# The small power-of-two products move from the output products' PSUM bank to columns of the transposes' banks

## The chip, the cores and the metric

One Trainium2 chip, one core. The metric is device time in microseconds; a kernel's time is the median of its runs. The engines are named as the profile names them: PE (TensorE, its matmuls), PEld (its weight loads), DVE (VectorE), ACT (ScalarE), POOL (GpSimd) and SP (SyncE, which here only issues DMAs).

## What is computed

Attention with a position bias, followed by a gated feed-forward block, all in fp32 (4 batches, 8 heads, 576 positions, head size 64; then 2304 tokens, 512 to 1536 to 512):

```python
scores = scale * np.matmul(q, k.transpose(0, 1, 3, 2))
x = (psi_rel / psi_i)[..., None]                       # log distances of positions
bias = np.maximum(x @ w1 + b1, 0.0) @ w2
scores = scores + bias.transpose(2, 0, 1)[None]
attn = np.exp(scores - np.max(scores, axis=-1, keepdims=True))
attn = attn / (np.sum(attn, axis=-1, keepdims=True) + 1e-09)
out = np.matmul(attn, v)                               # -> x: tokens by 512
return ((x @ w_a) * (x @ w_b)) @ w_out
```

## The kernel before

Attention goes by units (a batch, a pair of heads, one of two chunks of the queries), each cut into tiles of 128 queries by 576 keys. One generator, `attn_steps` (line 576), takes one step per tile `n` in two halves. The first half: `soft1(n)` (line 465; DVE line 472 adds the bias to the scores in PSUM and takes the extreme of each row, ACT line 477 takes the exponential), loads and preparations for coming units, and one step of `v_scale` (line 189). The second half: the scores of the next tile (`qk`, line 428, or `qk_pair`, line 450), `turn(n-2)` (line 514: five transposes of a finished tile on PE), where a unit is complete its output product (`pv_first`, line 480, or `pv`, line 547), and `soft2(n-1)` (line 500: POOL scales a tile by the reciprocal of its row sum).

`turn` allocates a PSUM tile `tp` of [128, 5, 128] fp32 from a pool with one buffer; PE fills its five columns of 128, then ACT copies all five to fp16 (line 538; for the first four units one plain copy, line 526), and DVE subtracts that copy to get the low parts (line 539 for columns 0 to 3, line 540 for partitions 64 to 127 of column 4). An output product fills a `pv` tile of [128, 512] fp32, also one buffer, which ACT (line 495 or 567) and then DVE (line 496 or 569) read out.

The weights of the feed-forward block and the values `v` are scaled by powers of two that are found on the chip. For that, ten times in all (six pairs of weight chunks, four batches of `v`), two small products are made: `pow2_down` (line 62) turns a column of maxima, one to four wide, into rows by a product with the identity (line 64, output 1 or 4 partitions by 128), DVE reduces it (line 66) and makes a small diagonal (lines 67 to 72); some steps later `pow2_up` (line 75) spreads that over 128 partitions by a product with ones (line 77, output 128 by 1 or 4), and DVE copies it out (line 79). Both take a `pv` tile under the name `pr`: they share the one buffer of the output products.

The weight steps (`wab_steps`, line 297: ACT and DVE build fp32 weights from 64-bit words, lines 244 to 249; ACT sums the absolute values, line 266; POOL and ACT split them into fp16 parts, lines 283 to 287), the feed-forward blocks (`moe_block`, line 635, products `ab` line 649; `moe_out`, products `o` line 698) and the attention steps are merged by count (lines 789 to 836). The order of PE's instructions is the order of the program (line 747). The order on the other engines is made by a planner from its own estimates; the program only adds that some instructions stay behind others (`late`, line 172) and that some loads stay behind the bias loads (`paced`, line 165). Waits between engines are put in by the framework from what each instruction reads and writes.

PSUM has eight banks of 512 fp32 values per partition: the scores take two, `tp` two, `pv` one, and three more the bias and first units at first and the feed-forward products later.

Of the kernel before, what the change touches and what calls it, by code (L numbers as in the profile page):

```python
# [7 lines left out]
F32 = mybir.dt.float32  # L8
# [39 lines left out]
def attention_moe(ctx, tc, q0d, q1d, kd, vd, idn, wp, wa, wb, wo, lsw, lg, rl, out):  # L48
# [8 lines left out]
    g_d = dram.tile([FC, 128, TOK], F32, name="g_d")  # L57
    winv = cst.tile([128, FC, 2], F32, name="winv")
    xt, cpool, epool, xpool = [], [None], [None], [None]
    vsc = []  # L60

    def pow2_down(mx, n, tag):
        ps = pvp.tile([128, 512], F32, tag="pv", name="pr")
        nc.tensor.matmul(ps[0:n, 0:128], mx, tab["idn"], start=True, stop=True)
        m = att.tile([n, 1], F32, tag="p2m" + tag, name="p2m", bufs=2)
        nc.vector.reduce_max(out=m, in_=ps[0:n, 0:128], axis=AX.X)
        nc.vector.tensor_scalar(out=m, in0=m, scalar1=3.0e38, scalar2=2.0 ** -100, op0=ALU.min, op1=ALU.max)
        nc.vector.tensor_scalar(
            out=m.bitcast(I32), in0=m.bitcast(I32), scalar1=0x7F800000, scalar2=None, op0=ALU.bitwise_and
        )  # L70
        dg = att.tile([n, n], F32, tag="p2d" + tag, name="p2d", bufs=2)
        nc.vector.tensor_scalar(out=dg, in0=tab["idn"][0:n, 0:n], scalar1=m, scalar2=None, op0=ALU.mult)
        return dg

    def pow2_up(dg, n, tag):
        ps = pvp.tile([128, 512], F32, tag="pv", name="pr")
        nc.tensor.matmul(ps[:, 0:n], tab["one"][0:n, :], dg, start=True, stop=True)
        g = att.tile([128, n], F32, tag="p2g" + tag, name="p2g", bufs=2)
        nc.vector.tensor_copy(g, ps[:, 0:n])
        return g  # L80
# [108 lines left out]
    def v_scale(b):  # L189
        mx = att.tile([128, NP], F32, tag="vmx", name="vmx", bufs=2)  # L190
        vfs = [load_v(b, hp) for hp in range(2)] if b else []
        yield
        for hp in range(NP):
            if b:
                junk = vf = vfs[hp]
            else:
                vf = st["vs", hp].rearrange("p x j d -> p (x j d)")
                junk = att.tile([128, 640], F32, tag="rv", name="junk", bufs=2)
            with late():
                nc.scalar.activation(junk, vf, AF.Abs, accum_out=mx[:, hp:hp + 1])  # L200
            junk = vf = None
            if b:
                vfs[hp] = None
                if hp + 2 < NP:
                    vfs.append(load_v(b, hp + 2))
            yield
        m1 = att.tile([128, 1], F32, tag="vm1", name="vm1", bufs=2)
        nc.vector.reduce_max(out=m1, in_=mx, axis=AX.X)
        dg = pow2_down(m1, 1, "v")
        yield  # L210
        if b:
            yield
        vsc.append(v_scales(pow2_up(dg, 1, "v"), b))
        yield
# [82 lines left out]
    def wab_steps(wt):  # L297
# [10 lines left out]
        for s in range(4 * np_ + 7):  # L308
            p, c = divmod(s - 7, 4)
            if 0 <= p < np_:  # L310
                if c == 0:
                    rms[p] = wab_scale(p, pow2_up(dgs.pop(p), 4, "w"))
                with late():
                    wab_parts(p, c, wfs.pop(s - 7), rms[p])
            p, c = divmod(s - 5, 4)
            if 0 <= p < np_ and c == 0:
                dgs[p] = pow2_down(ms.pop(p), 4, "w")
            if 1 <= s <= 4 * np_:
                p, c = divmod(s - 1, 4)
                if c == 0:  # L320
                    ms[p] = att.tile([128, 4], F32, tag="wm", name="wm", bufs=2)
                wab_size(2 * p + c // 2, c % 2, wfs[s - 1], ms[p])
            if s < 4 * np_:
                wfs[s] = wab_conv(*raws.pop(s))
                if s % 4 == 1 and s // 4 + 1 < np_:
                    fetch(s // 4 + 1)
            yield
# [186 lines left out]
    def turn(n, pool):  # L514
        u, t = TILES[n]
        c = UNITS[u][2]
        p = st.pop(("pn", n))
        tp = pool.tile([128, 5, 128], F32, tag="tp", name="tp", bufs=1)
        for x in range(5):
            c0 = min(128 * x, S - 128)  # L520
            nc.tensor.transpose(tp[:, x, :], p[:, c0:c0 + 128], tab["idn"])  # L521
        if u < NP:
            if t[0] == "A":
                st["pt", u] = epool[0].tile([128, 5, 256], F32, tag="pt", name="ptf", bufs=2)
            o = 128 * (t[0] == "B")
            evs.append(nc.scalar.copy(st["pt", u][:, :, o:o + 128], tp))
            return
        W = 512 + 128 * c
        if t in ("A0", "A2"):
            st["pt", u] = cpool[0].tile([128, 9, W], F16, tag="pt", name="pt", bufs=2)  # L530
        pt = st["pt", u]
        if t == "T":
            dst = pt.rearrange("p x (h w) -> p x h w", h=2)[:, :, :, 0:64]
            src = tp.rearrange("p x (h w) -> p x h w", h=2)
        else:
            o = {"A0": 0, "A1": 128, "B0": 256, "B1": 384, "A2": 64, "A3": 192, "B2": 384, "B3": 512}[t]
            dst, src = pt[:, :, o:o + 128], tp
        nc.scalar.copy(dst[:, 0:5], src)  # L538
        nc.vector.tensor_tensor(out=dst[:, 5:9], in0=src[:, 0:4], in1=dst[:, 0:4], op=ALU.subtract)  # L539
        nc.vector.tensor_tensor(  # L540
            out=dst[0:64, 4], in0=src[64:128, 4], in1=dst[64:128, 4], op=ALU.subtract
        )
# [33 lines left out]
    def attn_steps():  # L576
        vgen = [None]
        for n in range(NT + 3):
# [42 lines left out]
            if n >= 2 and n - 2 < NT:  # L621
                turn(n - 2, tpp)
# [120 lines left out]
    chunk_pool(0)  # L743
    qkp = ctx.enter_context(tc.tile_pool(name="qk0", bufs=1, space=PSUM))
    tpp = ctx.enter_context(tc.tile_pool(name="tp0", bufs=1, space=PSUM))
    pvp = ctx.enter_context(tc.tile_pool(name="pv0", bufs=1, space=PSUM))
    ctx.enter_context(tc.manual_schedule(engines={mybir.EngineType.PE}))
    wstack = ctx.enter_context(ExitStack())
# [140 lines left out]
```

## Time and profile before

| | |
|---|---|
| median of 3 runs | 876.42 us (870.93 to 877.58) |
| the profiled execution | 875.48 us, span 873.4 us |
| mean granted TensorE clock, of full speed | 0.945 |
| PE busy | 780.3 us (89%), 5936 matmuls |
| PEld busy | 622.9 us (71%) |
| DVE busy | 546.0 us (63%) |
| ACT busy | 512.5 us (59%) |
| POOL busy | 308.4 us (35%) |

The span is the time from the first to the last recorded instruction of the profiled execution. The busy time of an engine is the sum of its instructions; matmuls are pipelined, so a busy PE is not PE at its peak. In the timeline each row is a run of like instructions: the start in us from the span's start, the time that they took, the engine, the line, the operation, what is written from what, tile sizes, how many, and in brackets how long the engine was idle just before and whose end it then had waited for.

### The profile page before, as it was taken

The numbers are of one execution on the slowest core, as the hardware profiler recorded it, in microseconds if no ns is written. First come the engines' busy times: TensorE is split into PE (matmuls) and PEld (weight loads), VectorE is DVE, ScalarE is ACT, GpSimd is POOL, SyncE is SP. The second block draws the span as 40 slices with busy tenths as digits, with TensorE's granted clock in tenths as the row PEclk, the third lists the DMA queues.
The fourth block names the chain that finished last, engine by engine and source line by source line (L and its number), as shares of the span: only waits on it lengthen the run. The fifth ranks groups of instructions, "written<-read, shape, count | busy, mean of one in ns | idle before, by whom it ended". The sixth has DMA issues, their size and how long they took to land.

```text
span 873.4 us, 16482 instructions
## 1 busy us (share of the span) xinstructions
PE 780.3 (89%) x5936; PEld 622.9 (71%) x5936; DVE 546.0 (63%) x1291; ACT 512.5 (59%) x1102; POOL 308.4 (35%) x480
## 2 busy tenths in 40 slices
PE   5865669878888698988999999999999999999998
PEld 1244446647777466765888888888898898888886
DVE  5545577879799667765587778777787665210100
ACT  4747557857686467764577667766776666331310
POOL 0022446747366412321244433432443344220210
PEclk9959688969998799999999999999999999999999
DMA  7897265724776345443444444444443432100001
GB/s 214 242 298 237 77 217 185 208 60 126 232 231 186 91 141 163 139 120 100 127 126 130 130 139 147 118 133 137 117 121 125 127 87 65 55 2 25 1 10 39
DMA packets 52596, 114.16 MB, mean 131 GB/s; under 512 B 5156, under 2 KB 9508, under 8 KB 52516
## 3 DMA queue, kind: packets, MB, share of 16 engines
q1 hardware_dynamic: 44336, 97.34, 36.9%
q10 hardware_dynamic: 8180, 15.77, 6.1%
q8 instruction: 47, 0.77, 0.4%
q14 instruction: 33, 0.27, 0.1%
HBM read 95.91 MB, written 17.18 MB: 129 GB/s over the span
## 4 chain that ended last, share of the span: by engine, by line
PE 66%; DVE 11%; DMA 10%; ACT 6%; issue 4%; SPq 1%; POOL 1%; ACTq 0%; DVEq 0%; POOLq 0%
PE ab L649 25%; PE o L698 17%; PE tp L521 8%; PE qk L444 8%; PE pv L555 5%; PE psta L136 3%; DMA rv<-vd 2%; DMA wraw<-wb 2%; DVE p L472 2%; DMA bias<-bias_d 2%; ACT p L477 1%; DVE ks L373 1%; DVE wt L246 1%; DVE wt L249 1%; DMA rvf<-vd 1%
## 5 line engine op out<-in xcount | busy, mean ns | idle before, releaser
L649 PEld LDWEIGHTS <-w16t 128*128 128x128 f16 x2592 | 254.1, 99 | 44.2 <-issue 12.7
L649 PE MATMUL ab<-x,w16t 128*128 128x256 f16 x2304 | 276.5, 277 | 0.0
L472 DVE CUSTOM_DVE_ANT_0 p<-qk,bias 128x576 f32<-128x576 f32 x144 | 108.7, 755 | 90.4 <-PE tp L521 80.1
L508 POOL TENSOR_SCALAR p<-p,rc 128x576 f32<-128x576 f32 x144 | 126.5, 879 | 70.9 <-DVE rc L506 64.2
L538 ACT CAST pt<-tp 128x640 f16<-128x640 f32 x128 | 88.3, 690 | 101.9 <-PE tp L521 101.4
L477 ACT ACTIVATE p<-p,mn 128x576 f32<-128x576 f32 x144 | 111.7, 776 | 47.6 <-DVE mn L472 45.3
L521 PE MATMUL tp<-idn,p 128*128 128x128 f32 x720 | 111.7, 289 | 20.3 <-DVE pt L540 8.1
L505 POOL TENSOR_SCALAR rr<-sm 128x1 f32<-128x1 f32 x144 | 31.2, 217 | 278.0 <-ACT p L477 274.8
L698 PE MATMUL o<-wos,gh 128*128 128x512 f32 x384 | 124.4, 405 | 0.0
L674 POOL TENSOR_TENSOR gl<-g,gh 128x256 fp32r<-128x256 f32 x96 | 72.6, 758 | 132.0 <-ACT gh L673 130.8
L521 PEld LDWEIGHTS tp<-idn,p 128*128 128x128 f32 x720 | 87.8, 148 | 39.0 <-issue 19.9
L539 DVE TENSOR_TENSOR pt<-tp,pt 128x512 f16<-128x512 f32 x128 | 88.0, 688 | 8.6 <-ACT pt L538 8.3
L659 DVE SCALAR_TENSOR_TENSOR g<-ab,wv,asb 128x256 f32<-128x256 f32 x84 | 40.3, 482 | 82.2 <-ACT asb L657 80.9
L698 PEld LDWEIGHTS o<-wos,gh 128*128 128x128 f32 x384 | 69.1, 190 | 17.8 <-issue 5.4
L444 PE MATMUL qk<-ks,qs 128*128 128x288 f32 x384 | 73.2, 313 | 4.9 <-DVE mn L472 3.8
L698 PE MATMUL o<-wos,gl 128*128 128x512 f32 x192 | 75.8, 395 | 0.0
L136 PE MATMUL psta<-h,w2s 128*32 128x288 f32 (+17 forms) x352 | 48.7, 558 | 25.4 <-ACT bo L154 12.2
L444 PEld LDWEIGHTS qk<-ks,qs 128*128 128x128 f32 x384 | 57.3, 192 | 10.5 <-DVE mn L472 5.3
L657 ACT ACTIVATE asb<-ab,wv 128x256 f32<-128x256 f32 x84 | 39.2, 468 | 40.4 <-PE ab L649 40.3
L673 ACT CAST gh<-g 128x256 fp32r<-128x256 f32 x96 | 38.7, 405 | 35.1 <-DVE g L659 34.8
L555 PE MATMUL pv<-pt,vs 128*64 128x320 f16 (+1 forms) x784 | 56.5, 298 | 0.0
L126 DVE TENSOR_SCALAR h<-u,lgs 128x576 f32<-128x576 f32 (+17 forms) x117 | 46.4, 456 | 14.9 <-PE psta L136 14.5
(92 smaller groups left out, 977.0 us busy)
## 6 DMA issues: line engine op xcount, KB each, us to landing
bias<-bias_d SPq DMA_DIRECT2D x128, 288.0 KB
rv<-vd SPq DMA_DIRECT2D x40, 320.0 KB
bias_d<-bo ACTq DMA_DIRECT2D x36, 295.5 KB
rk<-kd SPq DMA_DIRECT2D x24, 288.0 KB
wraw<-wa SPq DMA_DIRECT2D x12, 512.0 KB
wraw<-wb SPq DMA_DIRECT2D x12, 512.0 KB
wraw<-wo SPq DMA_DIRECT2D x12, 512.0 KB
rq<-q1d SPq DMA_DIRECT2D x16, 320.0 KB
```

Of the source, the lines that this page charges most:

```text
L136: nc.tensor.matmul(dst[32 * g:32 * g + 32], tab["w2"], hs[g][:, c0:c1], start=True, stop=True)
L444: nc.tensor.matmul(ps[:, hf, :HB], a, b[:, hf * HB:hf * HB + HB], start=(x == 0), stop=(x == len(prods) - 1))
L472: ttr = nc.vector.tensor_tensor_reduce(out=p.rearrange("p (a n) -> p a n", a=2), in0=ps[:, :, :HB], in1=bt.rearrange("p (a n) -> p a n", a=2),
L477: exps.append(nc.scalar.activation(p, p, AF.Exp, bias=mn, scale=-1.0, accum_out=sm))
L508: nc.gpsimd.tensor_scalar(out=p, in0=p, scalar1=rc, scalar2=1.0, op0=ALU.mult, op1=ALU.mult)
L521: nc.tensor.transpose(tp[:, x, :], p[:, c0:c0 + 128], tab["idn"])
L538: nc.scalar.copy(dst[:, 0:5], src)
L539: nc.vector.tensor_tensor(out=dst[:, 5:9], in0=src[:, 0:4], in1=dst[:, 0:4], op=ALU.subtract)
L555: nc.tensor.matmul(ps[64 * j:64 * j + 64, :N], vs[:, part, vb, j, :], pt[:, pb, j * N:j * N + N], start=(x == 0), stop=(x == len(TERMS) - 1),)
L649: nc.tensor.matmul(ab[:, j], w16[nm, f][:, pw, kk, :], xs[px][:, kk, :], start=(x % (3 * KC) == 0), stop=(x % (3 * KC) == 3 * KC - 1),)
L674: nc.gpsimd.tensor_tensor(out=gl, in0=g, in1=gh.bitcast(F32), op=ALU.subtract)
L698: nc.tensor.matmul(o, g[:, sl], wos[f][:, p], start=(f == 0 and x == 0), stop=(f == FC - 1 and x == 2))
```

## The change

The two functions of the small products no longer allocate a `pv` tile. The `tp` tile is allocated once for the whole kernel with eight columns of 128 in place of five; `turn` writes and reads its columns 0 to 4, and the small products alternate between its columns 6 and 7. The pools and the number of banks that each takes stay as they are (a `tp` tile of five columns took two banks as well).

```diff
+    vsc, tpt = [], []
+    prs = [0]
+
+    def pr_tile():
+        prs[0] ^= 1
+        return tpt[0][:, 6 + prs[0], :]
 
     def pow2_down(mx, n, tag):
-        ps = pvp.tile([128, 512], F32, tag="pv", name="pr")
+        ps = pr_tile()
         nc.tensor.matmul(ps[0:n, 0:128], mx, tab["idn"], start=True, stop=True)
...
     def pow2_up(dg, n, tag):
-        ps = pvp.tile([128, 512], F32, tag="pv", name="pr")
+        ps = pr_tile()
         nc.tensor.matmul(ps[:, 0:n], tab["one"][0:n, :], dg, start=True, stop=True)
...
     def turn(n, pool):
...
-        tp = pool.tile([128, 5, 128], F32, tag="tp", name="tp", bufs=1)
+        tp = tpt[0][:, 0:5, :]
...
     tpp = ctx.enter_context(tc.tile_pool(name="tp0", bufs=1, space=PSUM))
+    tpt.append(tpp.tile([128, 8, 128], F32, name="tp"))
```

## Rows read from the trace of the kernel before

**Rows 1.** Stretches: length; busy us (and count) by engine; PE clock; DMA share; GB/s

```profile
50.00:134.00 84.00, 54.19 (x328) 37.53 (x328) 48.06 (x134) 49.88 (x115) 30.16 (x48) 0.74 0.64 208
134.00:290.00 156.00, 131.03 (x1015) 102.98 (x1014) 136.69 (x304) 112.32 (x239) 94.38 (x111) 0.90 0.57 170
290.00:874.00 584.00, 561.41 (x4414) 470.96 (x4414) 336.68 (x786) 321.99 (x685) 181.05 (x310) 0.99 0.34 100
```

**Rows 2.** Tile `pr` on PE: idle us before its products, how often, until what

```profile
  DVE x L496: 17.1, 5
  DVE x L569: 6.4, 2
```

**Rows 3.** Timeline: products of an `ab` tile's second half, and ACT reading the first

```profile
181.90 2.74 PE L649 MATMUL ab<-x,w16t 128*128 128x256 f16 x12
...
184.68 0.47 ACT L657 ACTIVATE asb<-ab,winv 128x256 f32<-128x256 f32 x1 [2.00 <-PE ab L649]
```

**Rows 4.** PE's timeline: small products that waited for `pv`, and one `qk`

```profile
88.48 0.58 PE L64 MATMUL pr<-idn,vm 128*1 128x128 f32 x2 [4.76 <-DVE x L496]
...
98.61 0.58 PE L77 MATMUL pr<-p2d,one 1*128 1x1 f32 x2 [3.56 <-DVE x L496]
...
112.70 2.29 PE L444 MATMUL qk<-rkf,rqf 64*128 64x288 f32 x4 [0.20 <-DVE mn L472]
...
130.26 0.58 PE L77 MATMUL pr<-p2d,one 4*128 4x4 f32 x2 [5.57 <-DVE x L496]
...
179.45 0.59 PE L64 MATMUL pr<-idn,wm 128*4 128x128 f32 x2 [5.89 <-DVE x L569]
```

**Rows 5.** Timeline of ACT and DVE: last reading of the `tp` tile before those

```profile
85.92 0.67 ACT L526 COPY ptf<-tp 128x640 f32<-128x640 f32 x1
...
94.77 0.68 ACT L526 COPY ptf<-tp 128x640 f32<-128x640 f32 x1
...
126.42 0.29 DVE L540 TENSOR_TENSOR pt<-tp,pt 64x128 f16<-64x128 f32 x1
...
175.33 0.29 DVE L540 TENSOR_TENSOR pt<-tp,pt 64x128 f16<-64x128 f32 x1
```

**Rows 6.** PE's waits, 130 to 290 us: us in total, times, longest

```profile
PE tp L521 <- DVE pt L540: 8.1, 5, 3.0
```

**Rows 7.** PE's timeline: up products (line 77) that stand behind transposes

```profile
146.14 0.38 PE L77 MATMUL pr<-p2d,one 4*128 4x4 f32 x2 [1.52 <-DVE p2d L72]
...
165.08 0.38 PE L77 MATMUL pr<-p2d,one 4*128 4x4 f32 x2
...
194.22 0.38 PE L77 MATMUL pr<-p2d,one 1*128 1x1 f32 x2
...
279.93 0.38 PE L77 MATMUL pr<-p2d,one 1*128 1x1 f32 x2
```

**Rows 8.** DVE's timeline: last reading of the `tp` tile before those four

```profile
147.29 0.29 DVE L540 TENSOR_TENSOR pt<-tp,pt 64x128 f16<-64x128 f32 x1
...
166.05 0.29 DVE L540 TENSOR_TENSOR pt<-tp,pt 64x128 f16<-64x128 f32 x1
...
196.80 0.29 DVE L540 TENSOR_TENSOR pt<-tp,pt 64x128 f16<-64x128 f32 x1
...
281.89 0.29 DVE L540 TENSOR_TENSOR pt<-tp,pt 64x128 f16<-64x128 f32 x1
```

**Rows 9.** Timeline: ACT's reading of `tp`, a down product, DVE's reading of `tp`

```profile
198.95 0.67 ACT L538 CAST pt<-tp 128x640 f16<-128x640 f32 x1
...
199.09 0.38 PE L64 MATMUL pr<-idn,wm 128*4 128x128 f32 x2 [1.11 <-ACT w16t L266]
...
203.16 0.29 DVE L540 TENSOR_TENSOR pt<-tp,pt 64x128 f16<-64x128 f32 x1
```

**Rows 10.** PE's timeline: the same eight score products at two times

```profile
77.87 1.31 PE L458 MATMUL qk<-rkf,rqf 64*128 64x288 f32 x8
...
100.08 2.29 PE L458 MATMUL qk<-rkf,rqf 64*128 64x288 f32 x8
```

More of the change, by code (lines that the diff above doesn't have):

```diff
@@ L59, in attention_moe @@
     xt, cpool, epool, xpool = [], [None], [None], [None]
-    vsc = []
+    vsc, tpt = [], []
[3 more added lines that the diff above has]
+        return tpt[0][:, 6 + prs[0], :]
     def pow2_down(mx, n, tag):
-        ps = pvp.tile([128, 512], F32, tag="pv", name="pr")
+        ps = pr_tile()
         nc.tensor.matmul(ps[0:n, 0:128], mx, tab["idn"], start=True, stop=True)
```

## The prediction

> **What bounds the kernel now.** I read the busy time of the engines by stretch first, then what the tensor engine (PE) waits for at the small products, then the timeline around each of them. By stretch [rows 1]: from 290 us on, PE is busy 561.41 of 584.00 us, and a microsecond that reaches 290 late reaches the end late. The change acts only before 290 us, where all the small products are. In 50 to 134 no engine is near its limit (PE 54.19, VectorE 48.06, ScalarE 49.88 of 84.00): this stretch is a chain of latencies. In 134 to 290 VectorE (DVE) is busy 136.69 of 156.00 us, PE 131.03: here PE is paced largely by what DVE hands back.
>
> PE runs its queue in the order written, so a small product that waits holds all that is queued behind it: the score products `qk`, the transposes `tp`, and from 134 us on the MoE products `ab`. All small products together cost PE 17.1 us of waiting for line 496 and 6.4 us for line 569, the second halves of the evacuation of `pv` [rows 2]. Those 23.5 us are what the change can take away at most by itself; the others of that list are waits for data (line 72, line 266) that stay.
>
> **The change, part by part.** Twenty small products (ten down, ten up) leave the `pv` bank. They get columns 6 and 7 of a `tp` tile which is now allocated once and has eight columns of 128. A bank holds 512 fp32 values in this kernel (`pv` and `ab` tiles are one such bank), so columns 0 to 3 are one bank and columns 4 to 7 the second. The fifth transpose writes column 4: the free blocks share its bank. Instructions, their sizes and their number stay the same.
>
> Does a small product then have to wait for the readers of column 4? The nearest row is line 657, which reads only the `a` half of an `ab` bank [rows 3]: ScalarE sat idle for 2.00 us and began when the twelve products at 181.90 for the `b` half of that bank had ended, though the `a` half was full before they began. So I take it that the program orders accesses by bank, not by column, and that the wait for `pv` is exchanged for a wait for the last reader of column 4. That is ScalarE's copy (line 526 or 538), and from unit 4 on also DVE's line 540, which reads partitions 64 to 127 of column 4. What changes is which evacuation is waited for.
>
> *Waits that shrink.* For each I compare the old start with the end of the new guard in the same profile. The product at 88.48 [rows 4] could start when the copy at 85.92 has ended, 86.59 [rows 5]: 1.9 us. At 98.61 the copy ends at 95.45: 3.2 us; a second product right behind it needs the first one's result read out, now as then, and follows at the same distance. At 130.26 the guard is line 540, over at 126.71: 3.6 us. At 179.45 line 540 is over at 175.62: 3.8 us. The other two of the five waits for line 496, 17.1 - 4.76 - 3.56 - 5.57 = 3.2 us together, I count at nothing: behind one of them the `qk` at 112.70 waits for line 472 and not for the product, and at the other ScalarE's queue has the copy behind the evacuation of `pv`, so that the guard comes no earlier. The second wait for line 569 is 6.4 - 5.89 = 0.5 us, and I leave it out. Sum: 1.9 + 3.2 + 3.6 + 3.8 = 12.5 us, of which 8.7 before 134 us.
>
> *The transposes.* Until now the whole `tp` tile had to be free. Now columns 0 to 3 need only the copy and line 539, and only the fifth transpose needs line 540. The transposes waited for line 540 five times in this stage [rows 6]; each can start its 0.29 us earlier: 1.5 us. The fifth transpose must also wait for the DVE instruction that reads the small product (66 or 79), which I cost at nothing: in the profile that read comes out before, or within, the four transposes ahead of it; without that cover it would be some tenths each.
>
> *Waits that are new.* A small product that stands shortly behind transposes had no wait for them and now gets one. Four up products write all 128 partitions and so meet line 540 for certain [rows 7, 8]: 146.14 would wait until 147.58 (1.4 us), 165.08 until 166.34 (1.3), 194.22 until 197.09 (2.9), 279.93 until 282.18 (2.3). Sum 7.9 us. Behind each stand `ab` or `qk` and then the next transposes, for which ScalarE's copy and line 472 wait.
>
> Three down products stand the same way, and the last is shown [rows 9]. They write one to four partitions. If only the copy holds it (over at 199.62) the one at 199.09 loses 0.5 us; if line 540 does (over at 203.45), 4.4 us. No row decides between them. I put the other two together between nothing and the same 4.4, because behind one of them the transposes waited for line 540 anyway. So the downs cost 0.5 to 8.8 us. Being undecided I take the middle, 4.6.
>
> The Trainium skill, "PSUM — Partial Sum Buffer", section "PSUM bank collisions raise a hardware error", bears on both halves of this. It asks that PSUM be guarded by bank and quadrant of 32 partitions and not by address, so disjoint columns do not make blocks free, which is what line 657's wait looks like too; and it allows different quadrants of a bank at the same time. By its quadrants the down products would miss line 540, and the raw sum would be -12.5 - 1.5 + 7.9 + 0.5 = -5.6 us; by whole banks it would be +2.7 us. No run here shows the quadrants.
>
> *The sum.* Raw: -12.5 - 1.5 + 7.9 + 0.5 = -5.6 us at one end, -12.5 - 1.5 + 7.9 + 8.8 = +2.7 at the other. The two stretches do not pass it on alike. The 8.7 us before 134 fall where no engine is full, and I let them through. The rest, -3.8 - 1.5 + 7.9 + 4.6 = +7.2 us, falls where DVE is at 88% and PE stands waiting for it in any case (8.1 us before transposes, [rows 6]); a PE that comes late there finds DVE's work already done, so I count half, +3.6. Net -8.7 + 3.6 = -5.1 us. The profiled execution took 875.48 us (span 873.4 and 2.1 around it), 0.9 below the median of 876.42; this gives 870.4 by the profile and 871.3 beside the median. I forecast **871 us**, a shade faster and inside 1%, which is about what a measurement of this kernel tells from no change.
>
> **Rivals.** *The clock gives the gain a second time.* After the long waits PE runs at the lower of its two clock levels: the same eight `qk` products took 2.29 us at 100.08 and 1.31 at 77.87 [rows 10], and the granted clock is 0.74 in 50 to 134 against 0.90 after it [rows 1]. Were the first stretch at 0.90, its 54.19 us of products would take 54.19 x (1 - 0.74/0.90) = 9.6 us less; half of it on the path is 4.8. With the later gains in full and the losses halved, (7.9 + 0.5)/2 = 4.2, it is -8.7 - 3.8 - 1.5 - 4.8 + 4.2 = -14.6 us, 862 beside the median. For it: the waits at 98.61 and 130.26 fall from 3.56 and 5.57 to 0.4 and 2.0 us. Against it: those at 88.48 and 179.45 keep 2.9 and 2.1, and the new waits may lower the clock elsewhere.
>
> *Slower: DVE's subtraction becomes the guard.* In 134 to 290 lines 539 and 540 stand in DVE's full queue, up to 3.5 us behind ScalarE's copy (from 199.62 to 203.16). If all seven later products wait for line 540, if none of it is absorbed, and if each wait is followed by one `qk` group at the low clock (2.29 - 1.31 = 1.0 us), the loss is 7.9 + 8.8 + 7 x 1.0 = 23.7 us against gains of 14.0: +9.7 us, some 886. For it: how late line 540 is in [rows 8, 9]. Against it: the early gains lie on the other stretch, and DVE has work to do meanwhile. It decides as soon as the guard of the down products is line 540 and DVE's order leaves the subtraction where it is.
>
> *The blocks are really free*, ordered by column. Then the 23.5 us go without any new wait: 17.1 in full and (6.4 + 1.5)/2 = 4.0, that is -21.1 us, 855. Against it stands line 657's wait.
>
> **Chances and range.** Mine 0.45 (its own range 866 to 880), the clock 0.30, the subtraction 0.21, free blocks 0.04. The instructions of DVE and ScalarE are ordered by the program's planner, which will order them anew, so even mine is worth several microseconds either way. The range takes in the clock rival, and the subtraction rival up to about its half: 858 to 885. Over 1% is 8.8 us here. Faster than that come the clock and the free blocks, 0.34, less what of the clock rival falls short, plus the lower edge of mine: 0.33. Slower comes the subtraction, and mine at its upper edge makes up for what falls short of it: 0.21. Within 1% remains 0.46.
>
> **What would show it.** Right: the small products in 80 to 135 us wait for line 526 or 540 in place of 496, together under about 5 us; at those of 146, 165, 194 and 280 PE has new waits for line 540 of 1 to 3 us; the up product now at 130.26 starts about 8 us earlier, and the stretch that begins at 290 keeps its length. If the granted clock in 50 to 134 rises to 0.85 or more, the clock rival is at work. If the small products between 134 and 290 wait over 12 us for line 540, it is the slower one; if they wait for no reader of `tp` at all, the last. I am wrong altogether if that last stretch changes its length, or if DVE's new order moves lines 245 to 249 ahead of what PE needs.

## The result: the changed kernel is slower by under 1%

The changed kernel took 884.3 us (median, 881.56 to 885.58) against 876.42; the ratio is 1.0092 with a 95% interval of 1.0063 to 1.0121. Measured once more beside later experiments it was 881.86 against 876.62, ratio 1.0053 (1.0023 to 1.0082). So it is a small loss, clear of no change, where I had forecast a gain of 5 us. The profiled execution has a span of 883.8 us, 10.4 more than before.

In the lines below, numbers of lines from 62 on are seven higher than before: 71 and 84 are the down and the up product (64 and 77), 545 to 547 the three readings of `tp` (538 to 540), 533 the copy of the first units (526), 574 and 576 the evacuation of `pv` (567 and 569). The small products stand under the name of the tile that they now write, `tp`.

The stretches of the changed kernel (columns as in [rows 1]):

```profile
50.00:134.00 84.00, 58.90 (x361) 40.41 (x360) 48.44 (x140) 53.91 (x124) 32.27 (x50) 0.73 0.67 208
134.00:290.00 156.00, 124.77 (x925) 95.64 (x922) 125.31 (x278) 101.56 (x218) 88.16 (x103) 0.87 0.54 163
290.00:883.00 593.00, 567.36 (x4471) 476.21 (x4471) 347.14 (x807) 329.04 (x700) 186.94 (x317) 0.99 0.34 101
```

By 134 us PE has done 361 products where it had done 328: the change is ahead there. In the next 156 us it does 925 instead of 1015 and falls behind. What it has not done by 290 is left for the end.

Some small products on PE's timeline of the changed kernel:

```profile
98.84 0.49 PE L84 MATMUL tp<-p2d,one 1*128 1x1 f32 x2
...
126.64 0.35 PE L84 MATMUL tp<-p2d,one 4*128 4x4 f32 x2 [0.19 <-ACT vs L414]
...
137.39 0.58 PE L71 MATMUL tp<-idn,wm 128*4 128x128 f32 x2 [3.17 <-DVE pt L547]
...
161.87 0.59 PE L71 MATMUL tp<-idn,wm 128*4 128x128 f32 x2 [5.72 <-DVE pt L547]
...
182.55 0.38 PE L71 MATMUL tp<-idn,wm 128*4 128x128 f32 x2 [1.69 <-ACT x L574]
...
198.54 0.55 PE L84 MATMUL tp<-p2d,one 1*128 1x1 f32 x2 [2.34 <-DVE pt L547]
...
207.15 0.59 PE L71 MATMUL tp<-idn,wm 128*4 128x128 f32 x2 [1.91 <-DVE pt L547]
```

The first two answer to the products at 98.61 and 130.26 in [rows 4]: their waits of 3.56 and 5.57 us are gone. The one at 182.55 answers to 179.45 there, and its 5.89 us have become 1.69. The three down products at 137.39, 161.87 and 207.15, one of which is that of [rows 9], had waited for nothing or for data of their own; now they wait 3.17 + 5.72 + 1.91 = 10.8 us for DVE's subtraction. PE's waits in the changed kernel from 134 to 296 us, in total, times, longest:

```profile
PE tp L71 <- DVE pt L547: 10.8, 3, 5.7
PE tp L84 <- DVE pt L547: 5.9, 3, 2.3
```

16.7 us of new waits stand there against the 23.5 us of [rows 2]. This is how the longest of them comes about (PE, ACT and DVE of the changed kernel):

```profile
155.38 0.77 PE L528 MATMUL tp<-idn,p 128*128 128x128 f32 x5
...
157.44 1.38 DVE L252 TENSOR_SCALAR wt<-wt 128x512 int32<-128x512 int32 x1
157.92 0.68 ACT L545 CAST pt<-tp 128x640 f16<-128x640 f32 x1
158.73 0.74 DVE L479 CUSTOM_DVE_ANT_0 p<-qk,bias 128x576 f32<-128x576 f32 x1
...
159.41 0.47 DVE L666 SCALAR_TENSOR_TENSOR g<-ab,winv,asb 128x256 f32<-128x256 f32 x1
...
159.81 0.67 DVE L253 SCALAR_TENSOR_TENSOR wt<-wraw,wt 128x512 int32<-128x512 int32 x1
...
160.40 0.41 DVE L252 TENSOR_SCALAR wt<-wt 128x512 int32<-128x512 int32 x1
...
160.74 0.68 DVE L546 TENSOR_TENSOR pt<-tp,pt 128x512 f16<-128x512 f32 x1
...
161.43 0.29 DVE L547 TENSOR_TENSOR pt<-tp,pt 64x128 f16<-64x128 f32 x1
```

The transposes are done at 156.1. ACT reads them at 157.92, and DVE runs the five others that are shown before its subtractions; the small product starts when line 547 has ended, though it writes other columns than that line reads. The partitions differ as well: the line reads 64 to 127, the product writes 0 to 3.

### The profile page after: what moved, and what is told of

It is laid out like the page before. It is cut to its first block, busy times and chain, and to the rows that moved or that the text cites. A ratio compares the mean times of both kernels' runs of the same rounds, so it can differ in the third digit from the quotient of the medians.

```text
span 883.8 us, 16594 instructions
## 1 busy us (share of the span) xinstructions
PE 785.1 (89%) x5936; PEld 624.0 (71%) x5936; DVE 545.5 (62%) x1291; ACT 513.1 (58%) x1102; POOL 310.1 (35%) x480
## 4 chain that ended last, share of the span: by engine, by line
PE 65%; DVE 11%; DMA 9%; ACT 7%; issue 4%; SPq 1%; POOL 1%; ACTq 0%; DVEq 0%; POOLq 0%
PE ab L656 25%; PE o L705 17%; PE qk L451 8%; PE tp L528 8%; PE pv L562 5%; DMA bias<-bias_d 3%; PE psta L143 3%; DVE p L479 3%; DMA rv<-vd 2%; ACT p L484 2%; DVE wt L253 1%; DVE wt L256 1%; DVE wt L252 1%; DVE g L666 1%; ACT w16t L293 1%
## 5 line engine op out<-in xcount | busy, mean ns | idle before, releaser
L656 PE MATMUL ab<-x,w16t 128*128 128x256 f16 x2304 | 279.7, 279 | 0.0
L681 POOL TENSOR_TENSOR gl<-g,gh 128x256 fp32r<-128x256 f32 x96 | 72.8, 760 | 130.0 <-ACT gh L680 128.7
L451 PEld LDWEIGHTS qk<-ks,qs 128*128 128x128 f32 x384 | 57.4, 192 | 10.6 <-DVE mn L479 5.4
```

The costliest lines, as they stand in the source:

```text
L451: nc.tensor.matmul(ps[:, hf, :HB], a, b[:, hf * HB:hf * HB + HB], start=(x == 0), stop=(x == len(prods) - 1))
L656: nc.tensor.matmul(ab[:, j], w16[nm, f][:, pw, kk, :], xs[px][:, kk, :], start=(x % (3 * KC) == 0), stop=(x % (3 * KC) == 3 * KC - 1),)
L681: nc.gpsimd.tensor_tensor(out=gl, in0=g, in1=gh.bitcast(F32), op=ALU.subtract)
```

## A table that locates it

Two products serve as marks: A is the up product of the second pair of weight chunks, the last small product before the first `ab` (130.26 before, [rows 4]); B is the up product of the last pair. What lies between them, and after B, comes from the profile of each kernel that was run (us):

| kernel: first eight / later twelve small products in | A | A to B | B to end | median of runs |
|---|---|---|---|---|
| before: pv / pv | 130.26 | 77.64 | 665.5 | 876.42 |
| changed: tp / tp | 126.64 | 90.65 | 666.5 | 884.3 |
| changed, again | 127.40 | 87.99 | 666.5 | 881.86 |
| e3: tp / pv | 122.41 | 77.85 | 665.8 | 868.98 |
| e4: pv / tp | 131.07 | 86.86 | 666.4 | 886.17 |
| e5: pv / pv, tp allocated once | 130.02 | 77.69 | 668.1 | 876.16 |
| e6: tp / tp, line 547 ahead of 546 | 128.68 | 90.44 | 667.2 | 881.97 |
| e1: only ups in tp | 127.60 | 83.38 | 666.6 | 881.04 |
| e2: only downs in tp | 130.04 | 82.93 | 666.7 | 881.07 |
| e7: own bank / pv | 115.82 | 75.21 | 665.1 | 861.42 |
| e8: own bank / ab | 113.71 | 75.15 | 664.1 | 854.65 |
| e9: own bank / tp | 114.74 | 89.23 | 666.8 | 872.16 |
| e10: tp / ab | 122.45 | 75.02 | 665.1 | 865.97 |

After B all thirteen agree within 4 us. Between A and B they fall into classes by where the later small products stand: 75 to 78 us when none is in the columns of `tp`, 83 when half of them are, 87 to 91 when all are. What happens before A changes nothing in that.

The same stretch from A to B, for the kernel before, the changed one, e4 and e3 (columns as in [rows 1]):

```profile
130.26:207.90 77.64, 64.23 (x428) 45.73 (x428) 63.38 (x151) 52.51 (x117) 46.60 (x56) 0.85 0.50 148
```

```profile
126.64:217.29 90.65, 70.64 (x429) 48.48 (x429) 66.52 (x158) 54.70 (x121) 49.34 (x58) 0.79 0.45 135
```

```profile
131.07:217.93 86.86, 71.74 (x429) 49.57 (x429) 63.07 (x152) 53.18 (x116) 46.77 (x56) 0.77 0.46 134
```

```profile
122.41:200.26 77.85, 61.61 (x429) 44.21 (x429) 64.55 (x158) 54.19 (x121) 49.48 (x58) 0.89 0.55 158
```

The changed kernel's 13.0 us are two things. PE's idle time grows from 77.64 - 64.23 = 13.4 to 90.65 - 70.64 = 20.0 us, by 6.6. And the same 429 products (428 are recorded before) take 70.64 instead of 64.23 us, 6.4 more, at a granted clock of 0.79 instead of 0.85. Behind the waits of 3.17, 5.72 and 2.34 us the products are slow; behind that of 1.26 us at 192.58 they are not. Here are twelve `ab` products of the changed kernel before its wait of 3.17 us and after it,

```profile
132.75 1.47 PE L656 MATMUL ab<-x,w16t 128*128 128x256 f16 x12
...
137.91 2.74 PE L656 MATMUL ab<-x,w16t 128*128 128x256 f16 x12
```

at granted clocks of 1.00 and 0.50, the upper and the lower of the two levels (2.4 and 1.2 GHz). The two parts need not be alike: in e4 PE's idle time grows by only 1.7 us, and the same products take 7.5 us more, at 0.77.

## The experiments

Two theories at first. The guard: a small product in the columns of `tp` waits for the last reader of their bank; early in the kernel that reader is prompt, later it is DVE's line 547, which is late. The planner: the order of DVE's, ACT's and POOL's instructions is made anew for every edit, and it is another order that costs the time. Ratios are to the kernel before, measured beside each run.

**e3: only the first eight in tp.**

```diff
     def pr_tile():
-        prs[0] ^= 1
-        return tpt[0][:, 6 + prs[0], :]
+        prs[0] += 1
+        if prs[0] <= 8:
+            return tpt[0][:, 6 + prs[0] % 2, :]
+        return pvp.tile([128, 512], F32, tag="pv", name="pr")
```

> Only the first eight small products (those before the first feed-forward products, four down and four up) use columns of the tp banks; the twelve later ones stay in the pv bank. The guard theory (the loss comes from products that wait for line 547, the DVE subtraction that reads column 4, after 134 us): the first ab product starts 4 to 6 us earlier than 134.12 us, PE waits for no line 547 before a small product after 134 us, and the time is 870 to 874 us, 2 to 6 below before. The planner theory (the loss comes from another order of DVE's, ACT's and POOL's instructions, which any edit brings): the time is above 880 us all the same. If the early gain is swallowed by the stretch paced by DVE, the time is that of before, 875 to 878.

868.98 us, ratio 0.9919 (0.9886 to 0.9951). The guard theory's case: the early part of the change is a gain of 7.6 us, a little more than expected, and it passes whole through the later stretch. The first `ab` product starts at 124.78, 9 us earlier.

**e4: only the later twelve in tp.** As e3, with `prs[0] > 8`.

> Only the twelve later small products use columns of the tp banks; the first eight stay in the pv bank. The guard theory: the gain of the first stretch is missing and the whole loss of the second is there, so it is slower than the changed kernel, 886 to 892 us, with waits for line 547 of 8 to 15 us in all before small products. The planner theory: about the changed kernel's 884, or nearer to before, with no relation to those waits.

886.17 us, ratio 1.0100 (1.0060 to 1.0140). The late part alone is the loss, and no smaller than that of the whole change. Its waits for the subtraction, total, times, longest, from 134 to 296 us:

```profile
PE tp L73 <- DVE pt L549: 6.8, 3, 3.5
PE tp L86 <- DVE pt L549: 6.5, 3, 2.3
```

13.3 us, inside the expected 8 to 15 (549 is line 547 here).

**e5: tp allocated once, nothing moved.** As e3, with every `pr` in the `pv` bank.

> All small products stay in the pv bank; only the tp tile is allocated once, with eight columns, for the whole kernel. The guard theory: no small product waits for a reader of tp, the transposes start up to 0.3 us earlier at five places, so 874 to 877 us. The planner theory: off by more than 4 us from before, in either direction.

876.16 us, ratio 0.9997 (0.9976 to 1.0019). One allocation for the whole kernel costs nothing and gains nothing that can be measured. Of the planner theory this run says nothing: in its trace DVE, ACT and POOL run all their instructions in exactly the order of before. What speaks against that theory are the other runs. Before, DVE runs 150 instructions between A and B. Compared one by one with that order, 67 of them stand elsewhere in e4, and 49 to 80 in e3, e7, e8 and e10, which are not slower there (75 to 78 us in the table above). Nor is DVE's subtraction later in the changed kernel: between 120 and 290 us it ends 3.2 us after the last of its transposes on average, where it was 3.7 before.

**e6: line 547 ahead of 546.**

```diff
+        nc.vector.tensor_tensor(
+            out=dst[0:64, 4], in0=src[64:128, 4], in1=dst[64:128, 4], op=ALU.subtract
+        )
         nc.vector.tensor_tensor(out=dst[:, 5:9], in0=src[:, 0:4], in1=dst[:, 0:4], op=ALU.subtract)
-        nc.vector.tensor_tensor(
-            out=dst[0:64, 4], in0=src[64:128, 4], in1=dst[64:128, 4], op=ALU.subtract
-        )
```

> The changed kernel with lines 546 and 547 written in the other order, so that DVE subtracts column 4 first. The guard theory: the guard of the late small products comes 0.7 us earlier at each of five waits (14.4 us in the changed kernel), 3 to 4 us in all, so 879 to 882 us. The planner theory: no gain that goes with the waits, 884 give or take 4. If DVE runs both lines back to back behind the same earlier work and that work is what is late, the gain is at most these 0.7 us each.

881.97 us, ratio 1.0059 (1.0030 to 1.0087); the changed kernel has 1.0092 and 1.0053, so the two times can't be told apart. The wait near 137 us stayed as it was (3.18), the one near 162 was 4.23, but it was 3.77 in the repeat of the changed kernel. The trace tells more than the time, because here line 546 reads column 4 and line 549 columns 0 to 3:

```profile
138.15 0.29 DVE L546 TENSOR_TENSOR pt<-tp,pt 64x128 f16<-64x128 f32 x1
138.46 0.69 DVE L549 TENSOR_TENSOR pt<-tp,pt 128x512 f16<-128x512 f32 x1
...
139.30 0.58 PE L71 MATMUL tp<-idn,wm 128*4 128x128 f32 x2 [3.18 <-DVE pt L549]
```

The product starts 0.15 us after line 549 has ended, and 0.85 us after line 546. It writes a column of the tile's second bank, and the reader that it waited for reads the first bank alone; the product at 163.90 shows the same. So this program orders accesses by the whole `tp` tile, not by bank. It shows the other way round as well: in the changed kernel the first of five transposes, which writes column 0, waits for the readout of a small product from column 6 or 7,

```profile
148.87 0.15 DVE L86 COPY p2g<-tp 128x4 f32<-128x4 f32 x1
...
149.17 0.74 PE L528 MATMUL tp<-idn,p 128*128 128x128 f32 x5 [0.86 <-DVE p2g L86]
```

The swap could bring no gain: whichever subtraction DVE runs last is the guard.

**e1 and e2: only the ups, only the downs.** In e1 `pow2_down` takes a `pv` tile as before, in e2 `pow2_up` does:

```diff
     def pow2_down(mx, n, tag):
-        ps = pr_tile()
+        ps = pvp.tile([128, 512], F32, tag="pv", name="pr")
```

> Only the ten up products (128 partitions written) use the tp banks; the ten down products stay in the pv bank. If every small product meets line 547's reading of the shared bank, ups late in the kernel wait as in the changed kernel, 1.3 + 2.3 + 2.3 = 5.9 us, while the down products behind transposes wait no more (10.8 us in the changed kernel); before 134 us the ups keep most of the gain (those that stood at 98.6 and 130.3). So 873 to 879 us, at least 4 us under the kernel with the downs alone. If the loss had to do with the order of the other engines, ups and downs would cost alike.

> Only the ten down products (1 or 4 partitions written) use the tp banks; the up products stay in the pv bank. If accesses are ordered by whole banks, as the changed kernel's trace looks, three of them wait for line 547 between 134 and 210 us, 9 to 11 us together, against some 4 us gained at the one near 180 us, and little is gained before 134 us: 879 to 887 us. If they were ordered by quadrants of 32 partitions, the downs would wait for ScalarE's copy alone and the time would be 870 to 876.

881.04 and 881.07 us, both with ratio 1.0059. e2 is as expected: the downs, which write one to four partitions, wait for DVE's subtraction, and not only for ScalarE's copy. In e2, DVE's subtraction and the product behind it:

```profile
162.33 0.29 DVE L547 TENSOR_TENSOR pt<-tp,pt 64x128 f16<-64x128 f32 x1
...
162.77 0.58 PE L71 MATMUL tp<-idn,wm 128*4 128x128 f32 x2 [5.11 <-ACT wt L251]
```

The profile puts this wait down to another instruction, but the product starts 0.15 us after line 547 has ended. e1 is a miss: I had expected the ups to be at least 4 us cheaper. Two of its rows on PE say why:

```profile
145.91 0.35 PE L84 MATMUL tp<-p2d,one 4*128 4x4 f32 x2 [3.56 <-DVE pt L547]
...
181.15 0.59 PE L71 MATMUL pr<-idn,wm 128*4 128x128 f32 x2 [5.97 <-DVE x L576]
```

An up that hardly waited in the changed kernel waits 3.56 us here, and the old wait of 5.97 us for `pv` near 180, which the whole change shortens, is still there. What a class of products costs is not a sum of its waits in another arrangement.

**e7: the first eight in a bank of their own.** Until the feed-forward products take their three banks, one bank is free. Made from the kernel before:

```diff
+    def pr_tile():
+        prs[0] += 1
+        if prp[0] is not None:
+            return prp[0].tile([128, 512], F32, tag=prp[1], name="pr", bufs=prp[2])
+        return pvp.tile([128, 512], F32, tag="pv", name="pr")
...
     with ... tc.tile_pool(name="eq", bufs=1, space=PSUM) as eq, tc.tile_pool(name="prb", bufs=1, space=PSUM) as prb:
+        prp[:] = prb, "pr", 1
...
+    prp[:] = [None]
     wop = ctx.enter_context(...)
```

> The first eight small products get a bank of their own (one is free until the feed-forward products take theirs); the twelve later ones stay in the pv bank; the tp tile is as before. If waits for readers of the shared bank are what the first eight still pay in the columns of tp (5.1 us for the copy in the run with the early ones alone), they go, and the time is 864 to 870 us, at or a little below that run. If what holds them there is data (the sums over v that wait for transfers), the time is that of that run, 866 to 872.

861.42 us, ratio 0.9846 (0.9810 to 0.9881), below the expected range: A comes at 115.82, 14 us ahead of before and 6.6 ahead of e3. On PE:

```profile
100.92 0.38 PE L71 MATMUL pr<-idn,wm 128*4 128x128 f32 x2
...
115.82 0.46 PE L84 MATMUL pr<-p2d,one 4*128 4x4 f32 x2
...
165.59 0.59 PE L71 MATMUL pr<-idn,wm 128*4 128x128 f32 x2 [6.23 <-DVE x L576]
```

The two that had waited 1.7 and 5.57 us for `pv` wait for nothing, and no transposes stand behind a DVE instruction that reads a small product. In the `tp` columns ACT's copy had been a guard with a cost of its own. In the changed kernel the first small product waited 3.48 us for it:

```profile
56.94 0.66 ACT L251 ACTIVATE wt<-wraw 128x512 f32<-128x512 f32 x1 [3.51 <-DMA wraw<-wa]
57.50 0.68 ACT L533 COPY ptf<-tp 128x640 f32<-128x640 f32 x1
...
58.24 0.59 PE L71 MATMUL tp<-idn,vm 128*1 128x128 f32 x2 [3.48 <-ACT ptf L533]
```

ACT has that copy behind a weight conversion which waits for a transfer. A product of PE thus came to wait for a load that it has nothing to do with.

**e8: own bank early, a rotating `ab` bank later.** As e7, and from the feed-forward products on `prp[:] = mps, "ab", 3`.

> As the run with the bank of their own, and the twelve later small products take one of the three rotating banks of the feed-forward products ab for the moment. PE never waits for such a bank before ab in the kernel before, so a free one is at hand: the 5.3 us that are left near 175 us before a down product go, no small product waits for a reader of tp or pv, and the time is 1 to 5 us under the run with only the early bank, 860 to 868 us. If instead a bank held for DVE's late reading of a small product keeps ab waiting, it is slower than that run by 2 us or more.

854.65 us, ratio 0.9761 (0.9737 to 0.9785): 2.4% faster than before, below the expected 860 to 868 us, and the best version of this study. No small product waits for a reader of `tp` or `pv`. Yet A to B is as long as in e7 (75.15 and 75.21): the wait of 6.23 us near 166 is gone, and a wait for data behind it grew,

```profile
158.49 0.38 PE L71 MATMUL pr<-idn,wm 128*4 128x128 f32 x2 [0.48 <-ACT w16t L273]
...
178.90 0.59 PE L71 MATMUL pr<-idn,wm 128*4 128x128 f32 x2 [3.97 <-ACT w16t L273]
```

The two profiles differ by 3.1 us of span, of which 2.1 lie before A; the medians differ by 6.8. Of the difference, 3.3 us are that e7's profiled execution (858.10 us) was the fastest of its four. Where the rest of e8's lead over e7 comes from is not settled by one profile of each.

**e9: own bank early, tp columns later.** e7 with `tp` allocated once and the later twelve in its columns 6 and 7.

> The first eight small products in a bank of their own, the twelve later ones in the columns of tp. If the early and the late part simply add up (the early bank took 15 us off, the late columns put 9.6 on), 869 to 873 us. If the late products wait for a DVE that is behind however early PE comes, the lead of the first stretch is waited away before the products near 137 and 162 us, those waits are longer than in the changed kernel, and the time is that of the changed kernel less a little, 878 to 885.

872.16 us, ratio 0.9949 (0.9922 to 0.9976). It adds up: each measured against the kernel before that ran beside it, e7 is 14.0 us faster and e9 4.5, so the late columns put 9.6 us on e7, as they put 9.6 on the kernel before. The theory that the late waits eat any lead has fallen, though its picture is there; PE comes 14 us earlier to the product that waits longest, and waits 6.51 us there in place of 5.72.

**e10: tp columns early, an ab bank later.** The changed kernel with `prp[0] = mps` for the later twelve, as in e8.

> The first eight in the columns of tp, the twelve later ones in a rotating bank of the feed-forward products. With no guard in the second stretch the early gain of the run with the early ones alone (869) comes through, and the late wait of 5.3 us for the pv bank goes as well: 859 to 866 us. If the late part of the run with both other banks gained only because its early part was so far ahead, 867 to 870.

865.97 us, ratio 0.9872 (0.9825 to 0.9919). The early gain stands, with or without the late `pv` waits; against e3 it is 3 us better, within what the two intervals allow for no difference.

**The changed kernel again.**

> The changed kernel as it is, beside the two others on the same chip: 881 to 887 us, its loss before small products in waits for line 547 of 10 to 17 us again.

881.86 us; its waits for line 547 before small products from 134 us on sum to 8.9 + 4.7 = 13.6 us.

**What stays open.** The first eight stand alike in the changed kernel, its repeat and e6 on the one side and in e3 and e10 on the other, and up to A the profiles show the same order of instructions on ACT, DVE and POOL (in e6 but for the two lines that it swaps). Still A comes at 126.6 to 128.7 in the former and at 122.4 in the latter; ACT waits longer there for loads of weights and of `v`: from 50 us to A 7.9, 10.6 and 10.7 us in all in the changed kernel, its repeat and e6, 6.0 and 4.7 in e3 and e10. Why these loads land later is not shown. It is part of why the pieces do not add up to the whole: -7.6 for e3 and +9.6 for e4 make +2, and the change measured +5 and +8. Between A and B the changed kernel is also slower than e4, by 3.8 us (1.1 in the repeat). Two things were not tried: a small tile of its own within the second bank of `tp`, and the late products in `tp` with DVE's subtraction moved ahead of the work that it stands behind.

## Why the prediction was wrong, by its steps

- *The order by bank* was right in that disjoint columns are not free, and wrong in its unit: the guard is the last reader of the whole `tp` tile, across both of its banks (e6). For the small products it comes to the same, since line 547 is the tile's last reader; the copy alone held no late down product. The Trainium skill, "PSUM — Partial Sum Buffer", section "PSUM bank collisions raise a hardware error", would let different quadrants of a bank be used at once; this program does not use that (a product to partitions 0 to 3 waits for a reader of 64 to 127), and no run here tried it.
- *The transposes*, -1.5, did not come. The first of the five still waits for line 547: at 132.17 in the changed kernel it starts 0.15 us after that line has ended. And the readout of the small products, costed at nothing, held transposes three times between A and B, 1.3 us together.
- *Waits that shrink*: 1.9 + 3.2 + 3.6 + 3.8. Before 134 us the sum came out in e3 (A is 7.9 us earlier, forecast 8.7), but by other parts. In the change itself A is only 3.6 us earlier (2.9 in the repeat), for the reason that stays open above. The product at 88.48 gained nothing, because data held it (4.46 us for the sum over `v`, behind a load); the one at 98.61 lost its whole wait. What was overlooked is the very first product, at 54.63 before, which had no wait and got one of 3.48 us; the step took only products that had waited for `pv`, and not those that stood free before 134 us.
- *Waits that are new*: the step that failed first. "Being undecided I take the middle, 4.6" for the down products: they waited 10.8 us, more than the upper end of 8.8, and 8.9 in the repeat. The ups came to 5.9 and 4.7 us against 7.9. Together 16.7 and 13.6, where I had 7.9 + 4.6 = 12.5.
- *Half of it absorbed*: the step that turned the sign. "A PE that comes late there finds DVE's work already done, so I count half, +3.6." The stretch from A to B became 13.0 us longer (10.4 in the repeat, 9.2 in e4), not 3.6. Of the new waits 14.4 us lie there; the `pv` wait of 5.89 us shrank by 4.2, and waits for data of 1.5 and 1.7 us went. That leaves 6.6 us more of idle time, unhalved, and 6.4 us of slower products came on top. A lower clock behind the waits stood only among the rivals, where it had one `qk` group, 1.0 us, for each wait; it belonged in the sum. By the profiles the whole is -3.6 us up to A, +13.0 from A to B and +1.0 behind B: +10.4 where the forecast had -8.7 + 3.6 = -5.1.
- *The rival that came true* is the slower one, with its place (lines 546 and 547 in DVE's full queue) and its deciding point (the downs' guard is the subtraction) and its sign (over 12 us of waits for it between 134 and 290 us: 14.4 there, 16.7 with one just behind). It was priced at 886; I gave it 0.21. Its reason against ("the early gains lie on the other stretch") holds too: e3 shows them.
- *The rival of free blocks*, 855 us, is wrong of the change, but e8, in which every small product does find a free bank, took 854.65.
- *After 290 us* the work takes as long as before, as forecast, if the cut is made at the same product: B to the end is 665.5 and 666.5. Cut at 290 us the last stretch is longer, because 57 more products are left for it.

## What to carry to other kernels

A free column of a shared PSUM tile is not a free place: in this program whoever writes it inherits the last reader of the whole tile, and that reader is late by what stands ahead of it in its engine's queue (in the longest case 5.7 us, behind five other instructions). Before moving a small product, list for each of its instances which reader it would meet and when that reader ends, also where it waited for nothing before; here one change was worth -7.6 us in one stretch and +9.6 in the next, and only the choice by stretch gains. And price a wait on PE at more than its length where it leaves the products behind it at the lower clock: 6.4 us came on top of 6.6 in the changed kernel, and 7.5 on top of 1.7 in e4.

## What the runs showed of the hardware

The cost of idle PE time was larger than I had expected. Between the same two products, 6.6 us more of idle time went with 6.4 us more for the same products, at a granted clock of 0.79 in place of 0.85; in e4 1.7 us more went with 7.5 us, at 0.77; in e3, where the stretch is as long as before with 2.8 us more idle time but in other places, the clock was 0.89 and the products took 61.61 us. So it isn't the sum of idle time alone that sets the clock.
